# Attention and MLP on one core: q and k of seven batches by way of fp16 copies in DRAM and DMA transposes

## The chip, the cores and the metric

The kernel runs on one core of a Trainium2 chip. A core has TensorE (PE: matmuls, whose weight loads stand apart as PEld), VectorE (DVE), ScalarE (ACT), GpSimd (POOL) and SyncE (SP). They run side by side and wait for one another on semaphores. In this kernel SP and POOL issue the DMAs. The metric is the device time of one execution in microseconds (us), as the median of several runs.

## The reference

```python
# q, k, v: (8, 12, 448, 64) float32: batch, heads, tokens, head size
scores = scale * np.matmul(q, k.transpose(0, 1, 3, 2))       # scale = 1/8
m = np.max(scores, axis=-1, keepdims=True)
e = np.exp(scores - m)
attn = e / (np.sum(e, axis=-1, keepdims=True) + np.exp(-m) + 1e-09)
attn_out = np.matmul(attn, v)
x = attn_out.transpose(0, 2, 1, 3).reshape(3584, 768)
h = x @ w_in                                                 # (768, 2048)
r = np.maximum(h, 0.0)
out = (r * r) @ w_out                                        # (2048, 768), float32 out
```

This is attention whose softmax has one more term in its sum (the exp(-m), which is exp(0) after the shift), and then an MLP with a squared ReLU over all 3584 tokens.

## The kernel before

Work is cut by batch (8), in each batch by pair of heads (6, so 48 pairs in all), and in each pair by key group (4 of 112 tokens). A batch has 448 tokens. The natural tiles have 112 partitions, and partition p holds tokens 4p to 4p+3; key group kk is the tokens 4p+kk. All matmul operands are fp16, so POOL's loads cast from fp32 (`load`, L78); the first three pairs of q and k come uncast through SP (`load_raw`, L86), so that they come soon.

For the scores, q and k must lie with the head size on the partitions. `regroup` (L102) makes a copy on DVE, for three pairs at a time and for q and k each, that puts the two heads of a pair side by side (`flatq`, `flatk`, L109). `transposes` (L114) then turns one pair with eight TensorE transposes (four of q, four of k, L119) into a PSUM tile of the pool of two `mp` buffers, and one DVE copy brings it to SBUF (`qkt`, L121): head 0 on partitions 0 to 63, head 1 on 64 to 127.

For each key group, `scores` (L124) issues two matmuls, one for each head (L128: weights 112 columns of k, moving operand 448 columns of q; head 0 in the upper 64 rows of the array and head 1 in the lower), and one ACT exponential of both (`et`, L129). DVE sums the four key groups (`es`, L133, L136). `values` (L138) multiplies with v (L141), `row_sums` (L144) sums over keys on TensorE (L147) and takes the reciprocal on ACT by a logarithm and an exponential (L150, L151), and `normalise` (L154) writes the pair's rows of `xt` on DVE (L158).

`mlp` (L161) is a generator that yields after each matmul. Its first part makes 16 blocks of the hidden layer: six matmuls (L167) into an `mp` buffer, a ReLU on DVE (`rt`, L172) and a square on DVE (`g`, L174). Its second part multiplies with w_out (L182), brings each result to SBUF on ACT (`ot`, L186) and stores it from SP (L196). Blocks have 384 or 512 tokens in turn, so that block b needs the batches up to b.

The order is written out by hand: the scheduler is off (L58), and each engine runs its instructions as the program issues them. The loop over pairs (L251) issues the scores of pair i, two key groups, then the transposes of pair i+1, then 45% of this pair's share of the MLP of the batch before (`drain`, L233), then the other two key groups, and then values, row sums and normalise of pair i-1 with the rest of the share in between. The share is a sixth of a block. So the first half of each batch holds the first product (L167) and the second half the second (L182). `regroup` of pairs 3 to 5 comes at the end of pair 1, that of the next batch's pairs 0 to 2 at the end of pair 4 (L294 to L297).

Loads of batch b+1 are issued on POOL at the start of batch b (L258; batch 1's at the start of the kernel, in halves, between slices of w_in, L212 to L221). The q and k tiles have two buffers, so POOL waits for DVE's regroup; v waits for L141.

Of the kernel before, what the change touches and what calls it, by code (L numbers as in the profile page):

```python
# [15 lines left out]
def kernel(  # L16
# [9 lines left out]
    nc = tc.nc  # L26
# [8 lines left out]
    P = S // RUN  # L35

# [7 lines left out]
    nat = ctx.enter_context(tc.tile_pool(name="nat", bufs=2))  # L44
    raw = ctx.enter_context(tc.tile_pool(name="raw", bufs=1))
    flat = ctx.enter_context(tc.tile_pool(name="flat", bufs=2))
    qkt_pool = ctx.enter_context(tc.tile_pool(name="qkt", bufs=3))
# [23 lines left out]
    nats, flats, xts = {}, {}, {}  # L71

    def tiles_of(b):
        if b not in nats:
            nats[b] = {n: nat.tile([P, H, RUN, D], FP16, name=f"{n}n") for n in ("q", "k", "v")}
        return nats[b]

    def load(b, names, p0, p1):  # L78
        hs = slice(2 * p0, 2 * p1)
        for n in names:  # L80
            r = {"q": q_r, "k": k_r, "v": v_r}[n]
            nc.gpsimd.dma_start(out=tiles_of(b)[n][:, hs], in_=r[b, :, hs])  # L82

    raws = {}

    def load_raw(b, p0, p1):  # L86
        hs = slice(2 * p0, 2 * p1)
        for n, r in (("q", q_r), ("k", k_r)):
            t = raw.tile([P, 2 * (p1 - p0), RUN, D], FP32, name=f"{n}raw{p0}")
            nc.sync.dma_start(out=t, in_=r[b, :, hs])  # L90
            raws[n, b, p0] = t
# [10 lines left out]
    def regroup(b, p0, p1):  # L102
        hs = slice(2 * p0, 2 * p1)
        n = 2 * (p1 - p0)
        both = []
        for name in ("q", "k"):
            t = raws.pop((name, b, p0)) if (name, b, p0) in raws else nats[b][name][:, hs]
            f = flat.tile([P, RUN, H // 2, D], FP16, name=f"flat{name}")
            nc.vector.tensor_copy(f[:, :, 0:n, :], t.rearrange("p h t d -> p t h d"))  # L109
            both.append(f)  # L110
        for pr in range(p0, p1):
            flats[b, pr] = both, 2 * (pr - p0)

    def transposes(b, pr):  # L114
        both, h0 = flats.pop((b, pr))
        tp = m_psum.tile([128, 2, 512], FP16, name="mp")
        for i, t in enumerate(both):
            for s in range(RUN):
                nc.tensor.transpose(tp[:, i, P * s:P * s + P], t[:, s, h0:h0 + 2, :], ident[0:P, 0:P])  # L119
        qkt = qkt_pool.tile([128, 2, S], FP16, name="qkt")  # L120
        nc.vector.tensor_copy(qkt, tp[:, :, 0:S])  # L121
        return qkt

    def scores(qkt, et, kk):  # L124
        sp = s_psum.tile([P, 2, 512], FP32, name="sp")
        for h in range(2):
            r = slice(64 * h, 64 * h + 64)
            nc.tensor.matmul(sp[:, h, 0:S], qkt[r, 1, P * kk:P * kk + P], qkt[r, 0, :], start=True, stop=True)  # L128
        nc.scalar.activation(out=et[:, kk], in_=sp[:, :, 0:S], func=AF.Exp, scale=scale)  # L129
# [7 lines left out]

    def values(b, pr, et, xp, kk):  # L138
        vn = nats[b]["v"]
        for h in range(2):  # L140
            nc.tensor.matmul(xp[64 * h:64 * h + 64, 0:S], vn[:, 2 * pr + h, kk, :], et[:, kk, h, :],  # L141
                             start=(kk == 0), stop=(kk == RUN - 1))

    def row_sums(es):  # L144
        zp = xz_psum.tile([128, 512], FP32, name="zp")
        for h in range(2):
            nc.tensor.matmul(zp[64 * h:64 * h + 64, 0:S], ones, es[:, 0, h, :], start=True, stop=True)  # L147
        lnz = z_pool.tile([128, S], FP32, name="lnz")
        rcp = z_pool.tile([128, S], FP32, name="rcp")
        nc.scalar.activation(out=lnz, in_=zp[:, 0:S], func=AF.Ln, bias=one_b)  # L150
        nc.scalar.activation(out=rcp, in_=lnz, func=AF.Exp, scale=-1.0)  # L151
        return rcp
# [8 lines left out]
    def mlp(t0, n):  # L161
# [15 lines left out]
        for ts in range(n // 128):  # L177
# [13 lines left out]
            while c < end:  # L191
                b, t, p = c // S, c % S // P, c % P
                m = min(P - p, end - c)
                o = c + 128 - end
                rows = out[b * S:(b + 1) * S, :].rearrange("(p t) m -> t p m", t=RUN)
# [3 lines left out]


    load_raw(0, 0, 1)
    load_raw(0, 1, 3)
    load(0, "v", 0, 3)
    load(0, "qk", 3, 6)
    load(0, "v", 3, 6)
# [8 lines left out]
    load(1, "qkv", 0, 3)  # L214
    for i in range(3, 6):
        load_win(i, 8)
    load(1, "qkv", 3, 6)
# [28 lines left out]
    qkts, ets, ess = {}, {}, {}  # L246
    regroup(0, 0, 1)
    qkts[0] = transposes(*pairs[0])
    regroup(0, 1, 3)
    share = 0.0  # L250
    for i in range(NP + 1):  # L251
# [3 lines left out]
        if i < NP:  # L255
            b, pr = pairs[i]
            if pr == 0 and 0 < b and b + 1 < B:
                load(b + 1, "qkv", 0, 6)  # L258
            et = ets[i] = e_pool.tile([P, RUN, 2, S], FP16, name="et")
            es = ess[i] = e_pool.tile([P, 2, 2, S], FP16, name="es")  # L260
            scores(qkts[i], et, 0)
            scores(qkts[i], et, 1)
            if i + 1 < NP:
                qkts[i + 1] = transposes(*pairs[i + 1])
            drain(share * 0.45)
            scores(qkts[i], et, 2)
# [3 lines left out]
            scores(qkts[i], et, 3)  # L270
            qkts.pop(i)
        if i > 0:
            for kk in range(2 if not work and i < NP else 0, RUN):
                values(*pairs[i - 1], ets[i - 1], xp, kk)
            rcp = row_sums(ess.pop(i - 1))
# [17 lines left out]
        if i < NP:  # L293
            if pr == 1:  # L294
                regroup(b, 3, 6)
            if pr == 4 and b + 1 < B:
                regroup(b + 1, 0, 3)  # L297
# [31 lines left out]
```

## Time and profile before

| What | Value |
|---|---|
| Three runs | median 497.36 us (495.08 to 498.45) |
| Profiled execution, its own time | 497.45 us |
| Its span | 495.7 us |
| Mean granted TensorE clock | 0.978 |
| Exponentials of the scores, ACT (L129) | 192 of 913 ns, 165.3 us busy |
| First product, PE (L167) | 768 matmuls, 163.6 us busy |
| Second product, PE (L182) | 896 matmuls, 153.9 us busy |
| Scores, PE (L128) | 384 matmuls, 62.3 us busy |
| Transposes, PE (L119) | 384 matmuls, 19.0 us (q) and 19.1 us (k) busy |
| Copies of the transposed pairs, DVE (L121) | 48 of 621 ns, 29.8 us busy |
| DMA bytes, packets | 34.97 MB, 45665 |

"Busy" is the time in which at least one instruction of the kind ran; matmuls overlap, so the mean of one times the count is more. In a timeline row stand the start, the time taken, the engine, the line, the operation, the tiles written and read, the shape and the count of merged instructions; a bracket at the end gives the engine's idle time before and what ended it. A windows row gives the length of a stretch, the busy time of each engine with its instructions, the mean granted clock, the DMA engines' share and the bytes moved.

Seen from the starts of the pairs' scores, batches last 55.4 us (3 and 5), 60.6 us (2 and 4), 53.0 us (1, from 43.7 us), 61.4 us (6) and 59.2 us (7); the MLP of the last block runs alone after that, from 449.3 us to the end.

### The profile page before, as it was taken

The numbers are of one execution on the slowest core, as the hardware profiler recorded it, in microseconds if no ns is written. First come the engines' busy times: TensorE is split into PE (matmuls) and PEld (weight loads), VectorE is DVE, ScalarE is ACT, GpSimd is POOL, SyncE is SP. The second block draws the span as 40 slices with busy tenths as digits, with TensorE's granted clock in tenths as the row PEclk, the third lists the DMA queues.
The fourth block names the chain that finished last, engine by engine and source line by source line (L and its number), as shares of the span: only waits on it lengthen the run. The fifth ranks groups of instructions, "written<-read, shape, count | busy, mean of one in ns | idle before, by whom it ended". The sixth has DMA issues, their size and how long they took to land.

```text
span 495.7 us, 7052 instructions
## 1 busy us (share of the span) xinstructions
PE 448.1 (90%) x2912; PEld 221.9 (45%) x2912; DVE 280.8 (57%) x532; ACT 244.2 (49%) x345; POOL 35.5 (7%) x46
## 2 busy tenths in 40 slices
PE   1787789997999979997999988998999989999996
PEld 1333345543355534543355534553345544455453
DVE  2656766457853568457754466637684277635800
ACT  2688436663355635663365635565245663561011
POOL 6342100001000010001000010000000000000000
PEclk9998999999999989999999989999899998999999
DMA  9999990256112580144702545115001210021022
GB/s 184 197 197 206 205 184 7 65 87 86 26 33 65 88 110 3 33 68 66 99 1 64 79 79 75 34 32 89 0 2 33 63 33 0 1 65 32 1 62 67
DMA packets 45665, 34.97 MB, mean 71 GB/s; under 512 B 1600, under 2 KB 42048, under 8 KB 45632
## 3 DMA queue, kind: packets, MB, share of 16 engines
q0 software_dynamic: 39744, 22.12, 33.1%
q1 hardware_dynamic: 5888, 12.39, 8.5%
q8 instruction: 23, 0.38, 0.3%
q14 instruction: 10, 0.08, 0.0%
HBM read 45.61 MB, written 11.01 MB: 114 GB/s over the span
## 4 chain that ended last, share of the span: by engine, by line
PE 73%; DVE 20%; ACT 3%; DMA 2%; issue 1%; SPq 0%; ACTq 0%
PE mp L182 30%; PE mp L167 20%; PE xp L141 9%; PE sp L128 8%; DVE rt L172 6%; PE mp L119 4%; DVE es L133 4%; DVE g L174 4%; DMA kraw<-in_k_dram 2%; PE zp L147 2%; DVE xt L158 2%; ACT et L129 2%; DVE es L136 2%; DVE qkt L121 2%; DVE flatq L109 1%
## 5 line engine op out<-in xcount | busy, mean ns | idle before, releaser
L129 ACT ACTIVATE et<-sp 112x896 f16<-112x896 f32 x192 | 165.3, 913 | 167.9 <-PE sp L128 167.9
L167 PE MATMUL mp<-xt,win 128*128 128x384 f16 (+1 forms) x768 | 163.6, 363 | 6.5 <-DVE rt L172 3.5
L182 PE MATMUL mp<-wout,g 128*128 128x512 f16 (+1 forms) x896 | 153.9, 326 | 0.4
L167 PEld LDWEIGHTS <-win 128*128 128x128 f16 x768 | 74.5, 100 | 86.2 <-issue 27.9
L182 PEld LDWEIGHTS <-g 128*128 128x128 f16 x896 | 84.9, 98 | 61.0 <-issue 9.2
L172 DVE TENSOR_SCALAR rt<-mp 128x384 f16<-128x384 f32 (+1 forms) x128 | 79.6, 622 | 56.4 <-PE mp L167 53.2
L133 DVE TENSOR_TENSOR es<-et 112x896 f16<-112x896 f16 x96 | 59.1, 622 | 83.0 <-ACT et L129 82.8
L128 PE MATMUL sp<-qkt 64*112 64x448 f16 x384 | 62.3, 395 | 4.3 <-ACT et L129 3.6
L186 ACT ACTIVATE ot<-mp 128x512 f32<-128x512 f32 (+1 forms) x56 | 27.3, 487 | 72.8 <-PE mp L182 72.1
L174 DVE TENSOR_TENSOR g<-rt 128x384 f16<-128x384 f16 (+1 forms) x128 | 50.1, 392 | 4.4
L141 PE MATMUL xp<-et,vn 112*64 112x448 f16 x384 | 49.7, 377 | 0.0
L121 DVE COPY qkt<-mp 128x896 f16<-128x896 f16 x48 | 29.8, 621 | 32.3 <-PE mp L119 32.3
L119 PE MATMUL mp<-ident,flatq 112*128 112x112 f16 x192 | 19.0, 226 | 28.9 <-DVE flatq L109 20.6
L128 PEld LDWEIGHTS <-qkt 64*112 64x112 f16 x384 | 19.2, 130 | 42.3 <-issue 40.0
L150 ACT ACTIVATE lnz<-zp,one_b 128x448 f32<-128x448 f32 x48 | 30.7, 640 | 4.1 <-PE zp L147 4.1
L158 DVE TENSOR_TENSOR xt<-xp,rcp 128x448 f16<-128x448 f32 x48 | 29.7, 619 | 4.8 <-ACT rcp L151 4.4
L119 PEld LDWEIGHTS <-flatq 112*128 112x128 f16 x192 | 11.5, 102 | 46.3 <-DVE flatq L109 29.5
L136 DVE TENSOR_TENSOR es<-es 112x896 f16<-112x896 f16 x48 | 29.9, 623 | 1.2
L141 PEld LDWEIGHTS <-vn 112*64 112x64 f16 x384 | 17.5, 111 | 24.5 <-issue 18.2
L151 ACT ACTIVATE rcp<-lnz 128x448 f32<-128x448 f32 x48 | 27.7, 577 | 1.5
L82 POOL DMA_DIRECT2D vn<-in_v_dram x10 | 9.0, 898 | 220.5 <-PE zp L147 217.2
L119 PE MATMUL mp<-ident,flatk 112*128 112x112 f16 x192 | 19.1, 228 | 2.6 <-DVE flatk L109 2.0
(20 smaller groups left out, 83.3 us busy)
## 6 DMA issues: line engine op xcount, KB each, us to landing
qn<-in_q_dram POOLq DMA_DIRECT2D x6, 672.0 KB, 7.8
kn<-in_k_dram POOLq DMA_DIRECT2D x6, 672.0 KB, 10.5
vn<-in_v_dram POOLq DMA_DIRECT2D x6, 672.0 KB, 8.9
win<-in_moe_w_in_dram POOLq DMA_DIRECT2D x8, 384.0 KB, 15.4
wout<-in_moe_w_out_dram POOLq DMA_DIRECT2D x4, 768.0 KB, 18.9
out_dram<-ot SPq DMA_DIRECT2D x8, 336.0 KB, 2.8
out_dram<-ot SPq DMA_DIRECT2D x8, 288.0 KB, 2.7
out_dram<-ot SPq DMA_DIRECT2D x8, 240.0 KB, 2.8
```

What stands on the lines that cost most here:

```text
L119: nc.tensor.transpose(tp[:, i, P * s:P * s + P], t[:, s, h0:h0 + 2, :], ident[0:P, 0:P])
L121: nc.vector.tensor_copy(qkt, tp[:, :, 0:S])
L128: nc.tensor.matmul(sp[:, h, 0:S], qkt[r, 1, P * kk:P * kk + P], qkt[r, 0, :], start=True, stop=True)
L129: nc.scalar.activation(out=et[:, kk], in_=sp[:, :, 0:S], func=AF.Exp, scale=scale)
L133: nc.vector.tensor_add(es[:, c], et[:, cs.start], et[:, cs.start + 1])
L136: nc.vector.tensor_add(es[:, 0], es[:, 0], es[:, 1])
L141: nc.tensor.matmul(xp[64 * h:64 * h + 64, 0:S], vn[:, 2 * pr + h, kk, :], et[:, kk, h, :], start=(kk == 0), stop=(kk == RUN - 1))
L158: nc.vector.tensor_mul(xts[b // 2][:, pr, c:c + S], xp[:, 0:S], rcp)
L167: nc.tensor.matmul(hp[:, 0:n], win[:, dc, fb * 128:(fb + 1) * 128], xt[:, dc, x0:x0 + n], start=(dc == 0), stop=(dc == DCH - 1))
L172: nc.vector.tensor_scalar(out=rt[:, 0:n], in0=hp[:, 0:n], scalar1=0.0, scalar2=None, op0=ALU.max)
L174: nc.vector.tensor_mul(g[:, 0:n], rt[:, 0:n], rt[:, 0:n])
L182: nc.tensor.matmul(op[:, 0:n1 - n0], gt[fb][:, ts * 128:(ts + 1) * 128], wout[:, fb, n0:n1], start=(fb == 0), stop=(fb == NFFB - 1))
```

## The change

Batch 0 keeps TensorE's transposes; its regroup is now one pair at a time, into buffers of the `g` pool, and its transposed q and k go to one tile `qk` of the whole batch. For each of batches 1 to 7, `stage` has POOL copy all of q and all of k of a batch from DRAM to DRAM with a cast to fp16, the k copy beginning 64 elements (one token) earlier than the batch. `transposed_loads` has SP load these copies with DMA transpose: a row of 128 elements is two tokens, so that even tokens land on partitions 0 to 63 and odd ones on 64 to 127. There are three loads for a batch: q, k, and k shifted by one token, so that each parity of keys is to be had on both halves of the partitions. `qk` has two buffers, one for each of two batches.

The scores of a key group of batches 1 to 7 are then four matmuls of 224 columns (each head, even and odd queries) in place of two of 448; their weights are read with a step of two columns. The tokens of a batch stand in the order even, then odd, through `et`, `es`, `xt` and the output, whose stores are cut accordingly (37 stores in place of 49). Issue order: batch 1's copies stand behind three slices of w_in on POOL, its v in one load behind three more; later batches' copies and v are issued where the loads were. The transposed loads of batch b+1 are issued on SP at the end of pair 2 of batch b. TensorE has as many instructions as before: 336 transposes fewer and 336 score matmuls more.

```diff
+    COLS = H * S // 2 + 16
-    nat = ctx.enter_context(tc.tile_pool(name="nat", bufs=2))
-    raw = ctx.enter_context(tc.tile_pool(name="raw", bufs=1))
-    flat = ctx.enter_context(tc.tile_pool(name="flat", bufs=2))
-    qkt_pool = ctx.enter_context(tc.tile_pool(name="qkt", bufs=3))
+    nat = ctx.enter_context(tc.tile_pool(name="nat", bufs=1))
+    v_pool = ctx.enter_context(tc.tile_pool(name="v", bufs=2))
+    qk_pool = ctx.enter_context(tc.tile_pool(name="qk", bufs=2))
...
+    HSD = H * S * D
+    FRONT, TOTAL = D, HSD + 16 * 2 * D
+
+    def stage(b):
+        for n, t in (("q", q), ("k", k)):
+            st = nc.dram_tensor(f"stage_{n}{b}", (TOTAL,), FP16, kind="Internal").ap()
+            stages[n, b] = st
+            src = t.rearrange("b h s d -> (b h s d)")
+            lo = b * HSD - FRONT
+            hi = min(lo + TOTAL, B * HSD)
+            m = (hi - lo) // 1024 * 1024
+            for x, y in ((lo, lo + m), (lo + m, hi)):
+                if y > x:
+                    w = min(y - x, 1024)
+                    nc.gpsimd.dma_start(out=st[x - lo:y - lo].rearrange("(r w) -> r w", w=w),
+                                        in_=src[x:y].rearrange("(r w) -> r w", w=w))
...
+    def transposed_loads(b):
+        qk = qks[b] = qk_pool.tile([128, 3, COLS], FP16, name="qk")
+        for i, n, x, c in ((0, "q", FRONT, H * S // 2), (1, "k", FRONT, H * S // 2), (2, "k", 0, COLS)):
+            nc.sync.dma_start(
+                out=qk[:, i, 0:c],
+                in_=stages[n, b][x:x + c * 2 * D].rearrange("(r c) -> r c", c=2 * D),
+                transpose=True,
+            )
+
+    def regroup(pr):
+        for j, name in enumerate("qk"):
+            f = g_pool.tile([128, 512], FP16, name=f"g{2 * pr + j}")
...
+        qk = qks[b]
+        if b == 0:
...
+        else:
+            for h in range(2):
+                for odd in range(2):
+                    r = slice(64 * odd, 64 * odd + 64)
+                    c = (2 * pr + h) * (S // 2)
+                    kc = c + kk // 2
+                    which = 1
+                    if kk % 2 != odd:
+                        which = 2
+                        kc += kk % 2
+                    nc.tensor.matmul(sp[:, odd, h * (S // 2):(h + 1) * (S // 2)],
+                                     qk[r, which, kc:kc + 2 * P - 1:2], qk[r, 0, c:c + S // 2],
+                                     start=True, stop=True)
...
+    def of_head(e, b, h):
+        if b == 0:
+            return e[:, h, :]
+        return e.rearrange("p o (h c) -> p h o c", h=2)[:, h]
...
-    load(1, "qkv", 0, 3)
+    stage(1)
     for i in range(3, 6):
         load_win(i, 8)
-    load(1, "qkv", 3, 6)
+    load_v(1, 0, 6)
...
-                load(b + 1, "qkv", 0, 6)
+                stage(b + 1)
+                load_v(b + 1, 0, NPAIR)
...
-            if i + 1 < NP:
-                qkts[i + 1] = transposes(*pairs[i + 1])
+            if i + 1 < NPAIR:
+                transposes(i + 1)
...
-            if pr == 1:
-                regroup(b, 3, 6)
-            if pr == 4 and b + 1 < B:
-                regroup(b + 1, 0, 3)
+            if i + 2 < NPAIR:
+                regroup(i + 2)
+            if pr == 2 and b + 1 < B:
+                transposed_loads(b + 1)
```

## The prediction

> **What bounds the kernel now.** I read the page first, engines and chain:
>
> ```profile
> PE 448.1 (90%) x2912; PEld 221.9 (45%) x2912; DVE 280.8 (57%) x532; ACT 244.2 (49%) x345; POOL 35.5 (7%) x46
> ...
> PE 73%; DVE 20%; ACT 3%; DMA 2%; issue 1%; SPq 0%; ACTq 0%
> ```
>
> TensorE is busy for 90% of the span, and the chain that ended last is PE with pieces of DVE in it. So two things pay: PE instructions that go, and PE idle time that DVE causes. The windows of two stretches, for block 4 (first matmuls, with PE clock) and block 3 (second matmuls), separate them:
>
> ```profile
> core 0: us, PE busy (x) PEld busy (x) DVE busy (x) ACT busy (x) POOL busy (x), PEclk, DMA share, GB/s
> 281.70:310.80 29.10, 25.30 (x165) 12.59 (x163) 20.42 (x43) 13.12 (x18) 1.86 (x2) 0.94 0.58 84
> 251.70:273.30 21.60, 21.60 (x153) 11.67 (x151) 9.93 (x18) 11.79 (x18) 0.00 (x0) 1.00 0.14 38
> ```
>
> While the second product runs, PE has no gap at all. While the first runs, 3.8 us of 29.1 are idle, and the clock is at 0.94. The timeline of PE and then of DVE shows where:
>
> ```profile
> 289.22 0.59 PE L128 MATMUL sp<-qkt 64*112 64x448 f16 x4
> 291.94 0.37 PE L119 MATMUL mp<-ident,flatq 112*128 112x112 f16 x4 [2.13 <-DVE flatq L109]
> 292.41 0.37 PE L119 MATMUL mp<-ident,flatk 112*128 112x112 f16 x4
> 292.61 4.43 PE L167 MATMUL mp<-xt,win 128*128 128x384 f16 x15
> ```
> ```profile
> 289.94 0.55 DVE L172 TENSOR_SCALAR rt<-mp 128x384 f16<-128x384 f32 x1
> 290.52 0.36 DVE L174 TENSOR_TENSOR g<-rt 128x384 f16<-128x384 f16 x1
> 290.80 0.62 DVE L158 TENSOR_TENSOR xt<-xp,rcp 128x448 f16<-128x448 f32 x1
> 291.33 0.55 DVE L109 COPY flatq<-qn 112x1536 f16<-112x1536 f16 x1
> 291.80 0.55 DVE L109 COPY flatk<-kn 112x1536 f16<-112x1536 f16 x1
> ```
>
> In the third pair of a batch PE wants to transpose, but DVE regroups q and k only behind its other work. PE waits 2.13 us. The same wait stands in all seven batches 1 to 7 (PE timeline: before 60.04, 115.58, 175.99, 231.54, 291.94, 347.52 and 408.82 us). The 15 matmuls behind it take 4.43 us; two batches earlier, with no wait before, the same number takes 2.60:
>
> ```profile
> 165.71 2.60 PE L167 MATMUL mp<-xt,win 128*128 128x384 f16 x15
> ```
>
> So a drop of the granted clock follows the wait. Transposes with nothing to wait for cost this:
>
> ```profile
> 312.00 0.58 PE L128 MATMUL sp<-qkt 64*112 64x448 f16 x4
> 312.51 0.37 PE L119 MATMUL mp<-ident,flatq 112*128 112x112 f16 x4
> 312.72 0.36 PE L119 MATMUL mp<-ident,flatk 112*128 112x112 f16 x4
> 312.92 2.54 PE L182 MATMUL mp<-wout,g 128*128 128x512 f16 x11
> ```
>
> Eight fill 312.51 to 312.92, 0.41 us. Four score matmuls of 448 columns fill 0.51 us.
>
> **The parts and their prices.** (1) Transposes go for pairs 6 to 47: 42 x 0.41 = -17.2 us. They lie on PE's path in both stretches.
>
> (2) The wait goes: 7 x 2.13 = -14.9. The flatk four start 0.47 us after the flatq four (291.94, 292.41), against 0.21 undisturbed: 7 x 0.26 = -1.8. What is late next is DVE itself: without the regroup it still has rt, g and xt to do until 291.33, and PE, with two mp buffers, can run about one and a half hidden blocks ahead (six matmuls, about 1 us each). I put back 0.4 us a batch, the size of the other mp waits in this stretch: +2.8. Bounds: 0, and the whole 16.7 if DVE holds PE just the same. DVE's load speaks for the low end: its 20.4 us busy in the 29.1 lose three qkt copies (0.62 each) and two regroup copies (0.55), so 17.4 is left, against a PE that needs some 22.3 (25.3 busy, less 1.2 of transposes and 1.8 of clock).
>
> (3) The clock: the 15 matmuls after the wait took 4.31, 4.40, 4.43 and 3.98 us in batches 1, 3, 5, 7 against 2.60, so 1.7 + 1.8 + 1.8 + 1.4; batch 6's third pair is 0.9 longer than those of batches 2 and 4. Together -7.6. Bounds: 0 (another gap trips it) to -7.6; I take all, since the only gap over 2 us in these batches is the one that goes.
>
> (4) PE waits 0.25 us for the qkt copy once a batch, because the transposes take one of the two mp buffers: -1.8. The 42 copies (0.62) and 22 of the 34 regroup copies leave DVE; beyond what is counted above they run beside PE and are worth nothing.
>
> (5) Scores of batches 1 to 7 become four matmuls of 224 columns instead of two of 448, in the same two row halves. The 15 matmuls from 165.71 to the next scores at 168.24 stream 15 x 384 columns in 2.53 us, 2.28 a ns. At that rate the four of 448 (a set: two key groups) would take 0.79 us one after another and 0.39 two at a time; they take 0.51. So they run two at a time, with 0.12 for the first load and the change of tile shape. So columns streamed stay the same. Weight loads double (336 more, with a step of two). Low bound 0; high bound, every further load exposed as the first is (a part of the 0.12, say 0.05): 84 sets (two for each of 42 pairs) x 3 x 0.05 = 12.6 us. I take +1, since L119 pays no visible load between matmuls of only 112 columns.
>
> [...]
>
> (6) Batch 0 keeps TensorE. Its regroup goes pair by pair, so three more iterations wait for DVE's xt and two copies before the transposes (up to about 1 us each), while the wait of 1.93 us before batch 1's transposes (39.57) goes. I call it even, within 3 us.
>
> (7) DMA. POOL's q and k loads of batches 1 to 7 (14 tensors) turn into casts from DRAM to DRAM of the same source bytes. They wait for no buffer that DVE frees (POOL now waits 61.2 us for flatq, which holds up nothing), so they are issued earlier, about a batch ahead. Batch 1's v becomes one load behind three of win: 5.7 MB into the queue, so at about 37 us plus what the transposed loads take, needed near 52.8, where L141 of batch 1's first pair runs. SP gets 21 transposed loads of 688 KB. Each waits for its copy and for the scores of two batches before; behind it on SP stand only stores, which wait for ScalarE anyway and are hidden behind two ot buffers. In steady state 2.1 MB of transposed loads a batch have about 50 us, as the copy runs a batch ahead. The first batch has less: the queues are full then.
>
> ```profile
> GB/s 184 197 197 206 205 184 7 65 87 86 26 33 65 88 110 3 33 68 66 99 1 64 79 79 75 34 32 89 0 2 33 63 33 0 1 65 32 1 62 67
> ```
>
> POOL's queue moves about 197 GB/s written. Before batch 1's copies stand 2.5 MB of POOL's loads (four of 336 KB, three of 384) and SP's 1.3 MB; with 1.35 MB of copies and the start, they land at about 28 to 30 us (5.2 MB / 197 + 2). Batch 1's scores begin at 43.66 us now. Nothing in the trace transposes by DMA. From below: by source bytes, 394 GB/s (the casts read twice what they write), 5.2 us for the three. From above, short of a collapse: the window of 12 to 40 us shows 10977 packets, 16 x 28 / 10977 = 41 ns each per engine; if each 256-byte row costs that, 3 x 168 x 41 ns = 20.7 us. Shared evenly with POOL's loads both double: 10.4 to 41 us, ending at 38 to 70, so a stall of 0 to 27 us, once. Nearest is the middle, moving bytes at 197 GB/s: 10.5, shared 21, ending near 47 to 49 if the first starts at 26. I take +3.
>
> [...]
>
> **Sum.** 495.7 - 17.2 - 14.9 - 1.8 + 2.8 - 7.6 - 1.8 + 1.0 + 0 + 3.0 = 459.2 us of span. The profiled execution took 497.45, 1.75 over its span, and equals the median of the runs (497.36). So 461 us.
>
> **Rivals.** A, the first batch starves: rows of 256 bytes cost 41 ns, batch 1 waits 12 to 27 us instead of 3: 470 to 485. For it: DMA is full for the first 74 us. Against it: only if arbitration gives SP's queue no more than half.
>
> B, DVE takes PE's place while the first product runs: the 16.7 and 7.6 us stay, less the 2.8 put back: 461 + 21.5 = 482. Against it: 17.4 us of DVE work in some 23.
>
> C, the transposed loads set the pace, and it is slower. They need 2.1 MB a batch; once that takes longer than a batch's PE work (about 50 us), the span is 26 + 7T + the last batch and tail (52 + 46). It equals 495.7 at T = 53 us, 17.7 us a load or 105 ns per row and engine. If a row is written in many small pieces, at 150 ns say, T is 76 and the time 26 + 529 + 98 + 1.75 = 655. Against it: the worst packet price seen is 41 ns, so it takes 2.6 times that. For it: nothing here shows such a load.
>
> D, the change does not do what it says: PE still waits as in B, and the scores' further loads are all exposed (11.6 more): 494, no change that can be told.
>
> **How the numbers follow.** The main case 0.62, A 0.10, B 0.07, C 0.17, D 0.04. The main case reaches from 451 (batch 0 gains 3, no stall, no DVE wait, no price of the scores) down to 449 for what these durations round, and up to 470, where A begins. The range 446 to 487 takes in the main case, A and B: 0.79. A measurement of this kernel tells about 1% from no change. Faster 0.79, same 0.04, slower 0.17; the main case's own range is 449 to 470.
>
> **What would show it.** Right: no L119 after 40 us; third pairs of 9.5 to 11 us instead of 13.3; score sets (eight matmuls) still 0.51 to 0.55 us; transposed loads landing within 25 us; odd batches near 49 us, even ones near 56, from 55.4 and 60.6. Wrong: PE waiting for DMA at the start of each batch (C) or of batch 1 alone (A); rt waits of 2 us at the third pair (B); score sets of 0.7 us (D).

## The result, and the profile after

The changed kernel is slower: 517.50 us (four runs, 514.19 to 520.34) against 497.90 (four runs of the kernel before, on the same chip), a ratio of 1.0394 with a 95% interval of 1.031 to 1.0477. The forecast was 461, and faster. The profiled execution took 517.9 us, with a span of 515.5; line numbers from here on are those of the changed kernel (scores of batches 1 to 7 L164, first product L211, second L226, copies to DRAM L112, transposed loads L121). The changed kernel issues 42 stores of the output where the kernel before issues 56.

The page first: engines, slices, DMA totals and the chain.

```profile
PE 426.3 (83%) x2912; PEld 219.7 (43%) x2912; DVE 242.0 (47%) x468; ACT 244.9 (48%) x345; POOL 29.4 (6%) x47
...
PE   2773000079999999999999999999999999999996
...
PEclk9998555569999999999999999999999999999999
...
DMA packets 84384, 49.50 MB, mean 96 GB/s; under 512 B 58688, under 2 KB 80320, under 8 KB 83904
...
PE 63%; DVE 15%; DMA 9%; another core or an unknown queue 8%; SPq 1%; POOL 1%; issue 1%; ACT 0%; POOLq 0%
```

TensorE did become cheaper: 426.3 us busy instead of 448.1, DVE 242.0 instead of 280.8. From the tenth slice on PE is at 9 in every slice but the last, where the kernel before falls to 7 or 8 time and again. But slices 5 to 8 (a slice is 12.9 us) are zeros, the granted clock falls to 0.5 there, and the chain has 9% of DMA and 8% of an unknown queue, where it had 2% of DMA. The waits of PE name the gap:

```profile
engine line waited for: us in total, times, longest us
PE sp L164 <- DMA qk<-stage_k: 59.9, 2, 42.7
...
PE mp L211 <- DVE rt L216: 5.7, 15, 0.6
```

Two waits at the start of batch 1 hold 59.9 us; no other wait for a transposed load is in the whole span, and 515.5 - 59.9 = 455.6. The PE timeline shows them, and SP's and POOL's timelines what was under way:

```profile
44.35 0.36 PE L191 MATMUL zp<-es,ones 112*64 112x448 f16 x2
61.91 0.43 PE L164 MATMUL sp<-qk 64*112 64x224 f16 x1 [17.20 <-DMA qk<-stage_k]
...
105.06 0.99 PE L164 MATMUL sp<-qk 64*112 64x224 f16 x7 [42.72 <-DMA qk<-stage_k]
```

```profile
26.18 7.07 SPq L121 DMA_TRANSPOSE qk<-stage_q  x1
33.29 66.05 SPq L121 DMA_TRANSPOSE qk<-stage_k  x2
100.74 4.58 SPq L121 DMA_TRANSPOSE qk<-stage_q  x1
105.41 5.79 SPq L121 DMA_TRANSPOSE qk<-stage_k  x2
```

```profile
40.16 0.52 POOL L112 DMA_DIRECT2D stage_q<-in_q_dram  x1 [2.48 <-DMA win<-in_moe_w_in_dram]
45.32 0.51 POOL L112 DMA_DIRECT2D stage_k<-in_k_dram  x1 [4.64 <-DMA vn<-in_v_dram]
```

Batch 1's three transposed loads (called T1 from here) start at 26.18 us, as forecast. The second one lands shortly before 62 us and the third shortly before 105, and not at 47 to 49. Meanwhile POOL issues batch 2's copies at 40 and 45 us. Batch 2's own transposed loads (100.74, 105.41) take 4.6 and 5.8 us on SP's queue. The copies are no earlier than what they replace: the kernel before issues batch 2's loads of q and k, beside which no transposed load stood, at 39 and 41 us:

```profile
39.19 1.34 POOL L82 DMA_DIRECT2D qn<-in_q_dram  x1 [1.71 <-DVE xt L158]
40.52 0.94 POOL L82 DMA_DIRECT2D kn<-in_k_dram  x1
```

After 112 us the kernel runs as forecast. Windows of a stretch with first products (batch 5) and of one with second products (batch 4):

```profile
core 0: us, PE busy (x) PEld busy (x) DVE busy (x) ACT busy (x) POOL busy (x), PEclk, DMA share, GB/s
320.50:349.10 28.60, 27.18 (x199) 14.16 (x198) 20.87 (x45) 15.27 (x21) 1.30 (x3) 1.00 1.00 157
289.60:312.40 22.80, 22.80 (x163) 12.50 (x160) 9.75 (x18) 12.65 (x20) 0.00 (x0) 1.00 0.12 35
```

PE idles 1.4 us of 28.6 where it idled 3.8 of 29.1, and the clock is 1.00 where it was 0.94. The third pair, where the 2.13 us wait and the 15 matmuls of 4.43 us behind it stood (the granted clock was 0.61 over those 4.43 us of the kernel before, and is 1.00 here from 327.58 to 331.59):

```profile
327.58 0.59 PE L164 MATMUL sp<-qk 64*112 64x224 f16 x8
328.11 0.50 PE L211 MATMUL mp<-xt,win 128*128 128x384 f16 x2
328.90 1.14 PE L211 MATMUL mp<-xt,win 128*128 128x384 f16 x6 [0.29 <-DVE rt L216]
330.29 1.30 PE L211 MATMUL mp<-xt,win 128*128 128x384 f16 x7 [0.26 <-DVE rt L216]
```

Batches from start to start of their scores, in us (for batch 7 its first five pairs), before and after; the last row is of the kernel that holds every copy, told of below:

| Kernel | 0 | 1 | 2 | 3 | 4 | 5 | 6 | 7 |
|---|---|---|---|---|---|---|---|---|
| before | 36.7 | 53.1 | 60.6 | 55.4 | 60.6 | 55.4 | 61.5 | 46.8 |
| changed | 55.1 | 91.3 | 55.0 | 49.1 | 55.0 | 49.1 | 55.0 | 41.1 |
| every copy held | 38.4 | 48.3 | 55.0 | 49.0 | 55.0 | 49.0 | 55.0 | 41.1 |

(The stall begins in the last pair of batch 0, whose time reaches to batch 1's first score.)

So the question is why T1, 2.07 MB, took 79 us. Counting the trace's single DMA packets by when they start gives this, with the mean time of one in brackets. SP's queue holds the rows of T1 (256 bytes each, 8080 of them for a batch), POOL's the others: 512 bytes for w_in and v, 1536 for w_out, 21632 for batch 2's copies. (Moving a stretch by some nanoseconds moves a count by a few.)

```
us        rows of 256 B    512 B         1536 B        21632 B
36-40     869 (31 ns)      870 (59 ns)
44-48     889 (32 ns)      799 (59 ns)   69 (137 ns)
56-60     456 (31 ns)                    447 (134 ns)
60-64     432 (31 ns)                    449 (134 ns)
68-72     178 (72 ns)                    74 (547 ns)   10 (1757 ns)
80-84     58 (495 ns)                    13 (1006 ns)  8 (2088 ns)
88-92     227 (325 ns)                   8 (564 ns)    6 (1612 ns)
100-104   332 (189 ns)                                 2 (1612 ns)   (287 of these rows behind the last packet)
104-108   3959 (20 ns)
108-112   3828 (20 ns)
```

Beside POOL's queue a row went for each packet of POOL's, at 512 bytes as at 1536: 870 packets to 869 rows, 447 to 456. Alone, from 104 us on, rows run at 3959 in 4 us: 253 GB/s, and that only where nothing else moves. Between 64 and 104 us far fewer rows come: few packets of either kind are under way, and all are slow. The end of that stretch, in quarters of a microsecond:

```
POOL's packets under way, 97 to 104 us: 97.07-98.68, 98.69-100.30, 100.33-101.94, 101.95-103.56 (21632 B each)
rows from 97.00: 38 7 0 0 | 0 0 1 17 | 0 0 0 0 | 0 14 18 0 | 0 0 0 1 | 12 0 0 0 | 0 0 27 260 | from 104.00: 281 275 263
```

Four packets, one after the other and so presumably on one of the 16 engines, let 13 to 32 rows through in each change of packets, about one or two for each engine if they lie evenly, and hardly any between (0 or 1 in a quarter); 0.2 us after the last of them the rate is 260 in a quarter. So would rows do that go on in step over the engines, at the pace of the engine with the most foreign packets: a conjecture, which the last experiment takes up.

### The profile page after: what moved, and what is told of

Read it like the earlier page. It is cut to its first block, busy times and chain, and to the rows that moved or that the text cites. A ratio compares the mean times of both kernels' runs of the same rounds, so it can differ in the third digit from the quotient of the medians.

```text
span 515.5 us, 7005 instructions
## 1 busy us (share of the span) xinstructions
PE 426.3 (83%) x2912; PEld 219.7 (43%) x2912; DVE 242.0 (47%) x468; ACT 244.9 (48%) x345; POOL 29.4 (6%) x47
## 3 DMA queue, kind: packets, MB, share of 16 engines
q0 software_dynamic: 21456, 22.18, 28.6%
## 4 chain that ended last, share of the span: by engine, by line
PE 63%; DVE 15%; DMA 9%; another core or an unknown queue 8%; SPq 1%; POOL 1%; issue 1%; ACT 0%; POOLq 0%
PE mp L226 29%; PE mp L211 17%; PE sp L164 8%; PE xp L185 7%; DVE rt L216 6%; DMA qk<-stage_k 6%; DMA stage_q<-in_q_dram 4%; DVE es L171 3%; DVE g L218 3%; PE zp L191 2%; SPq L121 1%; DVE es L174 1%; DVE xt L202 1%; POOL win L89 0%
## 5 line engine op out<-in xcount | busy, mean ns | idle before, releaser
L211 PE MATMUL mp<-xt,win 128*128 128x384 f16 (+1 forms) x768 | 158.4, 354 | 7.0 <-DVE rt L216 5.7
L226 PE MATMUL mp<-wout,g 128*128 128x512 f16 (+1 forms) x896 | 154.0, 326 | 0.4
L226 PEld LDWEIGHTS <-g 128*128 128x128 f16 x896 | 84.2, 98 | 63.6 <-issue 10.0
L211 PEld LDWEIGHTS <-win 128*128 128x128 f16 x768 | 71.8, 98 | 85.9 <-issue 24.9
L164 PE MATMUL sp<-qk 64*112 64x224 f16 x672 | 51.8, 273 | 60.6 <-DMA qk<-stage_k 59.9
L164 PEld LDWEIGHTS <-qk 64*112 64x112 f16 x672 | 32.2, 130 | 91.5 <-DMA qk<-stage_k 60.6
L194 ACT ACTIVATE lnz<-zp,one_b 128x448 f32<-128x448 f32 x48 | 30.7, 640 | 4.6 <-PE zp L191 4.6
L191 PE MATMUL zp<-es,ones 112*64 112x448 f16 x96 | 18.2, 376 | 0.0
L139 PE MATMUL mp<-ident,g 112*128 112x112 f16 x48 | 5.7, 297 | 14.4 <-DVE g L132 9.2
L152 PE MATMUL sp<-qk 64*112 64x448 f16 x48 | 12.9, 580 | 2.9 <-ACT et L167 2.2
L139 PEld LDWEIGHTS <-g 112*128 112x128 f16 x48 | 4.2, 139 | 17.9 <-DVE g L132 17.0
## 6 DMA issues: line engine op xcount, KB each, us to landing
win<-in_moe_w_in_dram POOLq DMA_DIRECT2D x8, 384.0 KB, 19.8
wout<-in_moe_w_out_dram POOLq DMA_DIRECT2D x4, 768.0 KB, 49.1
```

The lines of the kernel that those rows point to most:

```text
L164: nc.tensor.matmul(sp[:, odd, h * (S // 2):(h + 1) * (S // 2)], qk[r, which, kc:kc + 2 * P - 1:2], qk[r, 0, c:c + S // 2], start=True, sto ...
L191: nc.tensor.matmul(zp[64 * h:64 * h + 64, 0:S], ones, of_head(es[:, 0], b, h), start=True, stop=True)
L211: nc.tensor.matmul(hp[:, 0:n], win[:, dc, fb * 128:(fb + 1) * 128], xt[:, dc, x0:x0 + n], start=(dc == 0), stop=(dc == DCH - 1))
L226: nc.tensor.matmul(op[:, 0:n1 - n0], gt[fb][:, ts * 128:(ts + 1) * 128], wout[:, fb, n0:n1], start=(fb == 0), stop=(fb == NFFB - 1))
```

## The experiments

Theory P: T1 runs at its own speed only alone; beside POOL's queue each row waits for one of POOL's packets, so the size and number of the packets that POOL has queued set T1's end; everything else in the prediction stands. Rival B: T1 is slow because of the bytes that compete for the engines, so that only fewer bytes help. Rival for the other terms: the forecast's gain in the batches isn't due to the causes named.

All ratios are against runs of the kernel before on the same chip (median 497.90 for the changed kernel, 498.37 for the last two kernels, 498.02 for the others). The waits are those of the profiled execution.

| Kernel | us, median | ratio, 95% interval | PE's wait for transposed loads, us |
|---|---|---|---|
| changed | 517.50 | 1.0394, 1.031 to 1.0477 | 59.9, batch 1 |
| batch 2's copies held | 488.52 | 0.9802, 0.9755 to 0.9848 | 30.7, batch 1 |
| all POOL loads held for T1 | 480.87 | 0.9643, 0.9593 to 0.9692 | 19.8, batch 2 |
| copies in 832-byte packets | 492.88 | 0.988, 0.9836 to 0.9925 | 34.0, batch 1 |
| before, regroup a pair earlier | 483.93 | 0.970, 0.9649 to 0.9751 | none exist |
| every copy held | 458.63 | 0.9195, 0.9157 to 0.9232 | 0 |
| batch 2's copies held, thin w_out | 479.38 | 0.961, 0.9556 to 0.9664 | 21.1, batch 1; 7.6, batch 2 |
| every copy held, regroup in three | 457.02 | 0.9161, 0.9121 to 0.9201 | 1.4, batch 2 |
| the same, v first | 457.96 | 0.9193, 0.9144 to 0.9242 | 2.4, batch 2 |
| every copy held, one copy more | 459.57 (one run) | | 0.9, batch 2 |

**Batch 2's copies held.** POOL copies three numbers out of the tile that T1 fills, and so waits for T1 before it issues batch 2's copies. T1 is issued where it was on SP.

```diff
+    def fence():
+        mark = consts.tile([1, 3], FP16, name="mark")
+        nc.gpsimd.tensor_copy(mark, qks[1][0:1, :, 0])
...
     stage(1)
+    qks[0] = qk_pool.tile([128, 3, COLS], FP16, name="qk")
+    transposed_loads(1)
...
         load_wout(i, 4)
+    fence()
...
-            if pr == 2 and b + 1 < B:
+            if pr == 2 and 0 < b and b + 1 < B:
```

> The changed kernel, but POOL issues batch 2's copies only when batch 1's three transposed loads have landed (POOL copies three numbers of them first); the loads of w_in, v and w_out stand beside them as before. Theory P (the queues take turns packet by packet, so a transposed load of 256-byte rows advances one row for each packet of POOL's queue, and the 21632-byte packets of batch 2's copies starve it most): by 64 us some 5700 of 8080 rows are through as before, the rest runs beside the tail of w_out and then alone at about 990 rows a us, so batch 1's first scores start near 68 us in place of 105, and the time falls by about 36 us to 482. Rival H (the transposed loads are slow beside any traffic, and the size of the packets does not matter): the load ends near 90 us or later and the time stays above 500.

Measured 488.52 us, 6 above the 482 expected. The wait is halved, 30.7 us, and the second half of it goes from 42.7 to 13.3:

```profile
62.98 0.43 PE L164 MATMUL sp<-qk 64*112 64x224 f16 x1 [17.43 <-DMA qk<-stage_k]
76.71 0.99 PE L164 MATMUL sp<-qk 64*112 64x224 f16 x7 [13.30 <-DMA qk<-stage_k]
```

Batch 2's copies cost 29 us of the stall. The rest is w_in, v and w_out: up to 64 us the counts are those of the changed kernel (442 packets of 1536 bytes to 450 rows in 56 to 60). T1 ended at 76 and not some 8 us earlier: from 64 to 76 us the rows came at 898, 527 and 1029 in 4 us, beside POOL's last 259 packets (190, 47 and 22). Why they came so slowly beside so few was not shown.

**All POOL loads held for T1.** The same wait, but right behind batch 1's copies, so that nothing of POOL's runs beside T1. The rest of w_in, batch 1's v and w_out come after.

```diff
     stage(1)
+    qks[0] = qk_pool.tile([128, 3, COLS], FP16, name="qk")
+    transposed_loads(1)
+    fence()
     for i in range(3, 6):
         load_win(i, 8)
...
-            if pr == 2 and b + 1 < B:
+            if pr == 2 and 0 < b and b + 1 < B:
```

> The changed kernel, but POOL holds everything behind batch 1's copies (five slices of w_in, batch 1's v, w_out, batch 2's copies) until batch 1's transposed loads have landed. Theory P: the three loads run alone, at 253 GB/s as batch 2's did between 104 and 112 us, and land near 38 us, before batch 1 wants them at 44.7 us; no stall, w_out lands near 66 us, before it is wanted at about 72; time 455 to 460, as the steady batches (49 and 55 us) say. Rival W (the held weights come too late and PE waits for them instead): 465 to 480, with PE waiting for win or wout. Rival H: as the loads run nearly alone, no difference from P.

Measured 480.87 us, 21 us above what was expected, and the loss was in a place that no theory had. T1 landed at 39 us and batch 1 had no wait. But batch 2 waited. POOL's, SP's and PE's timelines:

```profile
39.09 0.26 POOL L249 COPY mark<-qk 1x3 f16<-1x3 f16 x1 [27.34 <-DMA qk<-stage_k]
49.78 0.52 POOL L112 DMA_DIRECT2D stage_q<-in_q_dram  x1 [1.30 <-DMA win<-in_moe_w_in_dram]
53.25 0.51 POOL L112 DMA_DIRECT2D stage_k<-in_k_dram  x1 [2.94 <-DMA vn<-in_v_dram]
57.53 0.50 POOL L112 DMA_DIRECT2D stage_q<-in_q_dram  x1 [0.94 <-DMA win<-in_moe_w_in_dram]
61.78 0.50 POOL L112 DMA_DIRECT2D stage_k<-in_k_dram  x1 [3.75 <-DMA wout<-in_moe_w_out_dram]
```

```profile
76.04 26.62 SPq L121 DMA_TRANSPOSE qk<-stage_q  x1
102.76 8.15 SPq L121 DMA_TRANSPOSE qk<-stage_k  x2
```

```profile
110.63 0.43 PE L164 MATMUL sp<-qk 64*112 64x224 f16 x1 [17.92 <-DMA qk<-stage_k]
112.91 0.99 PE L164 MATMUL sp<-qk 64*112 64x224 f16 x7 [1.85 <-DMA qk<-stage_k]
```

POOL went on to issue batch 3's copies at 57.5 and 61.8 us, behind batch 2's, and they ran beside batch 2's transposed loads: the q load alone occupies SP's queue for 26.6 us. It is the same collision one batch later.

**Copies in 832-byte packets.** Order of the changed kernel; only the copies' rows are cut, so that a packet has 832 bytes (1024 in the last batch) instead of 21632. Bytes stay the same, so this tells P from B.

```diff
-            for x, y in ((lo, lo + m), (lo + m, hi)):
-                if y > x:
-                    w = min(y - x, 1024)
...
+            w = 416 if hi - lo == TOTAL else 512
+            for j in range(2):
+                nc.gpsimd.dma_start(out=st[0:m].rearrange("(r j w) -> r j w", j=2, w=w)[:, j],
+                                    in_=src[lo:lo + m].rearrange("(r j w) -> r j w", j=2, w=w)[:, j])
```

> The changed kernel, but each copy from DRAM to DRAM is two, of alternate pieces of 416 elements (832 bytes written; 512 elements in the last batch), so that no packet is larger than 1536 bytes; order and waits are those of the change. Theory P: the rows no longer meet packets of 21632 bytes; after 64 us the last 2300 rows run at 110 to 215 rows a us and end at 75 to 85 us; time 488 to 500. Rival D (copies from DRAM to DRAM collide with the transposed loads whatever their packets): batch 1 starts as late as now, 510 to 525.

Measured 492.88 us, within what P expects. With the same bytes in the same order the wait falls from 59.9 to 34.0 us:

```profile
61.34 0.43 PE L166 MATMUL sp<-qk 64*112 64x224 f16 x1 [15.22 <-DMA qk<-stage_k]
80.56 0.99 PE L166 MATMUL sp<-qk 64*112 64x224 f16 x7 [18.79 <-DMA qk<-stage_k]
```

Rows again come one for one: from 72 to 76 us 616 rows beside 568 packets of 832 bytes and 23 of 1536. It is the size of the packets, and B falls.

**The kernel before, regroup a pair earlier.** The other side of the prediction: is the wait for `flatq` at the third pair worth what terms 2 and 3 say? In the kernel before, and there alone, the regroup of pairs 3 to 5 moves from the end of pair 1 to that of pair 0.

```diff
-            if pr == 1:
+            if pr == 0:
                 regroup(b, 3, 6)
```

> The kernel before, with one edit: the regroup of pairs 3 to 5 is issued at the end of a batch's first pair instead of its second. Theory: the wait of 2.13 us at the third pair of batches 1 to 7 and the clock drop behind it come only from where the regroup stands in DVE's order; without it 14.9 + 1.8 + 7.6 us less up to 2.8, so 473 to 478. Rival: DVE is the bound of that half in any case, and PE waits elsewhere for it: 488 to 497.

Measured 483.93 us, 14 us less than before and not 20 to 25. The 2.13 us wait and the clock's drop are gone (the clock is 0.9 or more from the sixth slice on, and 1.00 from 278 to 306 us), but two smaller waits stand in the third pair instead:

```profile
284.66 0.36 PE L119 MATMUL mp<-ident,flatq 112*128 112x112 f16 x4 [0.73 <-DVE rt L172]
284.85 0.36 PE L119 MATMUL mp<-ident,flatk 112*128 112x112 f16 x4
285.05 0.49 PE L167 MATMUL mp<-xt,win 128*128 128x384 f16 x2
286.12 2.27 PE L167 MATMUL mp<-xt,win 128*128 128x384 f16 x13 [0.58 <-DVE qkt L121]
```

The transposes still take one of the two mp buffers and DVE still has to empty it. So 14 of the 39 us that the change is worth without its stall (next kernel) can be had with one moved line; the rest was seen only with the transposes and their copies off PE and DVE.

**Every copy held.** As with all POOL loads held for T1, and from batch 2 on POOL also waits for a batch's transposed loads before it issues the next batch's copies.

```diff
             if pr == 0 and 0 < b and b + 1 < B:
+                if b > 1:
+                    fence(b)
                 stage(b + 1)
                 load_v(b + 1, 0, NPAIR)
```

> As e2 (POOL holds all behind batch 1's copies until batch 1's transposed loads have landed), and in each later batch POOL also holds the next batch's copies until the current batch's transposed loads have landed. In e2 batch 2's first scores still waited 18 us, because batch 3's copies ran beside batch 2's transposed loads. Theory P: with no packet of 21632 bytes beside any transposed load, no batch waits for DMA; from e2's own starts 44.4 + 48.3 + 55.0 + 49.0 + 55.0 + 49.0 + 55.0 + 99.4 = 455 us of span, time 457 (455 to 460), ratio about 0.92. Rival L (the copies now start too late and each batch waits for its transposed loads): some us more in each of batches 3 to 7, 465 or more.

Measured 458.63 us, ratio 0.9195. This is the changed kernel without its stall, and it beats both. POOL's timeline shows its waits; SP's shows T1; and the page shows PE:

```profile
39.58 0.59 POOL L250 COPY mark<-qk 1x3 f16<-1x3 f16 x1 [27.23 <-DMA qk<-stage_k]
...
91.90 0.18 POOL L250 COPY mark<-qk 1x3 f16<-1x3 f16 x1 [34.88 <-DMA qk<-stage_k]
```

```profile
26.53 3.66 SPq L121 DMA_TRANSPOSE qk<-stage_q  x1
30.24 7.03 SPq L121 DMA_TRANSPOSE qk<-stage_k  x2
```

```profile
PE 425.3 (93%) x2912; PEld 219.2 (48%) x2912; DVE 241.8 (53%) x468; ACT 245.0 (54%) x345; POOL 31.7 (7%) x53
...
PE   2677899999999999999999999999999999999996
...
PEclk9996799999999999999999999999999999999999
```

T1 alone takes 26.5 to about 39 us. PE has no wait for a transposed load in the whole span, nor one for w_in, w_out or v, so what POOL holds back is not missed.

**Batch 2's copies held, thin w_out.** The order of "batch 2's copies held", and w_out cut by columns in three parts, so that its packets are of 512 bytes and not 1536. By P T1 gains, by bytes it can't.

```diff
-        w = NFFB // n
-        nc.gpsimd.dma_start(out=wout[:, i * w:(i + 1) * w, :], in_=wout_r[:, i * w:(i + 1) * w, :])
+        w = DM // n
+        nc.gpsimd.dma_start(out=wout[:, :, i * w:(i + 1) * w], in_=wout_r[:, :, i * w:(i + 1) * w])
```

> As e1 (only batch 2's copies are held), but w_out is loaded in three parts of 256 columns, so that its packets are 512 bytes written in place of 1536, for the same bytes. Theory P (one packet of each queue in turn): beside w_out the transposed loads advance at the 215 to 240 rows a us that they had beside w_in's 512-byte packets, in place of 112; from 48 us, with some 3700 rows to go, they end near 64 to 66 us in place of 75, and the time falls by 8 to 10 us from e1's 488.5, to 478 to 481. Rival B (the queues share by bytes or by time): the size of POOL's packets changes nothing, 487 to 490.

Measured 479.38 us, as P has it: three runs are between 478.5 and 479.9, and the ratio is theirs. The profiled execution took 488.89 and also waits 7.6 us at batch 2, so its trace is used for T1 alone. There T1 is through at 66 us instead of 76, and rows and packets go one for one to the end: 951 packets of 512 bytes to 963 rows from 56 to 60 us, where "batch 2's copies held" had 442 of 1536 to 450.

**Every copy held, regroup in three.** Term 6: batch 0's regroup in two groups (pairs 0 to 2 ahead of the loop, pairs 3 to 5 at the end of pair 1) in place of one pair at a time.

```diff
+    regroup(2)
...
-            if i + 2 < NPAIR:
-                regroup(i + 2)
+            if i == 1:
+                for later in range(3, NPAIR):
+                    regroup(later)
```

> As e5, but in batch 0 the regroup copies of pairs 1 and 2 are issued together and those of pairs 3 to 5 together at the end of pair 1, as in the kernel before, in place of one pair at a time. The change's batch 0 reached its last pair at 40.5 us (e2: 38.9) where the kernel before did at 36.7. Theory: it is DVE's order that costs this (each iteration's transposes wait for the copies behind normalise), so 2 to 4 us come back against e5. Rival: batch 0 is bound by its loads, no difference from e5 (within 1 us).

Measured 457.02 us against 458.63, with intervals that overlap: inconclusive. In the profiled execution, which at 458.71 us was the slowest of the six, batch 1 starts 3.3 us earlier (41.9 against 45.2; with batch 0 as it was, two other kernels start it at 44.4 and 43.3, so the gain is 1.4 to 3.3). But the second interval between its pairs is 11.67 us instead of 8.88, and v is what is late:

```profile
54.57 0.95 PE L185 MATMUL xp<-et,vn 112*64 112x448 f16 x8 [1.64 <-DMA vn<-in_v_dram]
```

**The same, v first.** Batch 1's v is loaded directly behind the wait, ahead of the held slices of w_in.

```diff
+    load_v(1, 0, 6)
     for i in range(3, 6):
         load_win(i, 8)
-    load_v(1, 0, 6)
```

> The regrouping of batch 0 with batch 1's v loaded ahead of the held slices of w_in. If the wait for v at 54 us is what ate the gain of the regrouping (second interval of batch 1 11.7 us against 8.9, and the clock drop behind it), the second interval returns to about 9 us, and the time is 2 to 3 us below the run before it: 454 to 455.5. Rival: the slices of w_in come late in v's place, a wait of PE for them stands in batch 1, and the time stays at 457.

Measured 457.96 us: what neither expected. The wait for v is gone, and the second interval is back at 8.88 us, and no wait for w_in has come in its place. But batch 2, which batch 1 now reaches at 90.41 us instead of 93.46, waits for its transposed loads:

```profile
90.41 0.30 PE L164 MATMUL sp<-qk 64*112 64x224 f16 x1
93.10 0.99 PE L164 MATMUL sp<-qk 64*112 64x224 f16 x7 [2.39 <-DMA qk<-stage_k]
94.03 3.71 PE L226 MATMUL mp<-wout,g 128*128 128x512 f16 x15
```

These loads are issued at 76.31 to 77.33 us in all three kernels and are through by 91.9 to 94.8, since their copies stand behind everything that POOL held back for T1. So an earlier batch 1 meets the next wait in this order of issue; batch 3 begins at 148.5 to 149.7 us in all three. The 15 matmuls behind the wait take 3.71 us instead of 2.56; behind the gap in the kernel before it was 4.43 instead of 2.60.

**Every copy held, one copy more.** A test of the step "in step over the engines": 17 more packets of 21632 bytes, from v to a scratch in DRAM that nothing reads, on POOL's queue behind batch 1's copies.

```diff
     transposed_loads(1)
+    aside = nc.dram_tensor("aside", (17, 12032), FP16, kind="Internal").ap()
+    far = v.rearrange("b h s d -> (b h s d)")[0:17 * 12032].rearrange("(r w) -> r w", r=17)
+    nc.gpsimd.dma_start(out=aside[:, 0:10816], in_=far[:, 0:10816])
     fence(1)
```

> The version that holds every copy, with one more copy on POOL's queue beside batch 1's transposed loads: 17 packets of 21632 bytes into a scratch in DRAM that nothing reads. If the rows of a transposed load go on together over all DMA engines (theory S), a few large packets on few engines slow all rows: some tens to a few hundred rows in 4 us while the copy runs instead of 2500 to 2800, and batch 1's first scores wait for it, 5 to 20 us. If each engine takes its own rows by itself (rival I), the rows run at over 2000 in 4 us at first, only those of the engines concerned are late, and a wait at batch 1 is no longer than the packets of one engine, under 5 us.

One run, 459.57 us. As a stall it failed: 16 of the packets ran beside one another before T1 had begun in earnest, so batch 1 did not wait, and neither theory's time is tested. The packets themselves still bear on it. The last one, 28.05 to 29.66 us, is the only one under way after 28.92. Rows started in each quarter of a microsecond:

```
from 28.00: 156 136 86 36 | from 29.00: 18 9 7 150 | from 30.00: 285 283 282 285
```

With this single packet under way all rows together die down to 7 in a quarter, and they are back when it ends at 29.66. But this is the start of a load, and a load's start looks like this by itself: the second load of "the same, v first", with no packet of another queue under way, begins at 31.68 with 78, 109, 173, 219, 147, 34, 28 and 229 rows in its first quarters. So this run does not decide.

Two other traces do, in the midst of a load. There one packet of 16384 bytes of the instruction queue is under way, and no other packet but the rows: from 90.04 to 91.14 us in "the same, v first", and from 375.09 to 376.24 in the changed kernel. Rows started in each quarter:

```
from 90.00: 269 160 10 0 | from 91.00: 4 9 9 109 | from 92.00: 283 284
from 375.00: 242 265 75 2 | from 376.00: 1 8 9 10 | from 377.00: 236 287
```

If one packet is on one of the 16 engines, which no record shows, engines that went by themselves would have kept 15 of 16 of the rows. The rows return 0.6 to 0.8 us after the packet's end. With no other packet under way or ended less than 1 us before, the middle of a load (from 2.25 us after its first row to 0.5 us before its last) never falls below 277 rows in a quarter, in eight of the traces. So the stretch of the changed kernel from 97 to 103.6 us is not an accident of that place.

## Why the prediction was wrong, point by point

**The step that failed is (7)**, in the words "Shared evenly with POOL's loads both double: 10.4 to 41 us, ending at 38 to 70, so a stall of 0 to 27 us, once. Nearest is the middle". The stall came once, at batch 1, and was 59.9 us. Three things were wrong in it:

- "Shared evenly" was taken by time. The queues shared by packets: 869 rows of 256 bytes to 870 of POOL's packets of 512, 456 to 447 of 1536. Copies in packets of 832 bytes in place of 21632 took 26 us off the stall; with batch 2's copies held, w_out in packets of 512 in place of 1536 took 9 us off the time.
- Beside a single packet of another queue the rows of a load all but stopped: 0 to 10 in a quarter of a microsecond beside one of 16384 bytes, against some 280. This nothing in the trace of before could have shown. That the rows wait for the slowest engine, and that this made the stretch from 64 to 104 us slower than turns taken by each engine for itself, is the author's reading; no record names an engine.
- The copies from DRAM to DRAM were not priced as a neighbour of T1. The working has them "issued earlier, about a batch ahead", because no buffer of DVE's holds them. They were not: batch 2's were issued at 40.16 and 45.32 us, where the kernel before issued its loads at 39.19 and 40.52, and batch 3's, with all POOL loads held for T1, at 57.53 and 61.78, where the kernel before had 60.28 and 61.20. What was new is that T1 stood beside batch 2's copies, with their packets of 21632 bytes. Holding these copies alone took 29 us off.

The size alone: T1 by itself takes about 12 us (26.5 to 39), against a taken 10.5. With POOL's queue held back, the span is 455.6 us; the sum without its 3 us of stall gives 456.2.

**Rivals.** A had the right mechanism, batch 1 alone starving, and named its condition ("only if arbitration gives SP's queue no more than half"), but priced it at 12 to 27 us by the same even sharing, and gave it 0.10. C asked for 105 ns a row and engine all the way; between 80 and 84 us a row did take 495 ns, but only in the start. Later the same collision is there and hidden: batch 3's q load, beside batch 4's copies, occupies SP's queue from 160.91 us for 13.61, and is needed at 208. B and D are refuted by the third pair (waits of 0.29 and 0.26 us) and by the score sets. No rival joined A's mechanism with a price past the break-even: from 459.2 of span, 3 of them stall, 39.5 us of stall sufficed to make the kernel slower.

**The other terms.** The forecast of (1) to (5) together was -39.5 us. In the kernel that holds every copy, batches 1 to 7 (for 7 five pairs) are 40.8 us shorter by the table above, and the last pair with what follows 0.8: -41.6. These 2.1 us more than forecast make up for the 1.6 by which batch 0 ends later there, so the closeness of the whole sum is in part luck.

- (1) to (4): odd batches 49.05 us after, even ones 55.03; forecast "near 49" and "near 56". Only their sum is tested, not each price. The removed wait and the clock's drop are not from the transposes' absence alone: moving one regroup gave 14 us in the kernel before.
- (2), the 0.4 us a batch put back: 0.29 + 0.26 = 0.55 in batch 5.
- (3): the clock is 1.00 in the stretches that had 0.94.
- (5): a set of eight score matmuls of 224 columns takes 0.52 us (row below), where four of 448 took 0.51. The further weight loads cost at most 84 x 0.01 = 0.8 us; the +1 was right. The later matmuls of the set start two at a time, 96 ns a pair (319.62, 319.71, 319.81), so 48 ns each.

```profile
319.48 0.59 PE L164 MATMUL sp<-qk 64*112 64x224 f16 x8
320.00 2.61 PE L211 MATMUL mp<-xt,win 128*128 128x384 f16 x15
```

- (6): where batch 1 does not stall, batch 0 ends between 0.3 us earlier and 1.6 later (43.34, 44.40 and 45.22 in three kernels, against 43.66), within the 3 allowed. Grouping the regroup gains 1.4 to 3.3 us there, which later waits for loads take back.

The sum with the stall as measured is 459.2 - 3 + 59.9 = 516.1 of span, against 515.5.

## What to carry to other kernels

When a change makes a transfer urgent that was not there before, list what other queues have under way beside it: large transfers that were harmless there can now hold up the kernel, as batch 2's copies did here (holding them back took 29 us off). Price a transfer of many small rows beside another queue by the other queue's packets (rows per engine times the time of one packet, an estimate that gives 3.2 of the 4 us from 36 and 3.8 of the 4 from 56 here; and more beside large packets, where one of 16384 bytes left 0 to 10 rows in a quarter of a microsecond), not by bytes; and if it is needed soon, hold the other queue back until it has landed. Here six such waits, one for each of batches 1 to 6, turned 4% slower into 8% faster.

## What the runs showed of the hardware

- A transposed load and POOL's queue took turns one packet each: in 4 us 870 packets of 512 bytes to 869 rows, 447 of 1536 to 456, and 568 of 832 with 23 of 1536 to 616. Equal counts alone would fit turns of several packets each too; 13 to 32 rows for each 21632-byte packet (97 to 104 us) do not, if they lie evenly over the 16 engines: the turn was one or two rows. Where many such packets are under way at once (164 to 170 us, batch 3's loads beside batch 4's copies) it is 12 to 18 rows beside 14 to 17 packets in 2 us.
- With one packet of 16384 bytes of another queue under way in the midst of a load, 0 to 10 transposed rows started in a quarter of a microsecond instead of some 280 (two traces). The cause stays open: that the rows go on in step over the engines was not shown. The packets' records do not name their engine, so that the four packets from 97 us on shared one engine is read from their following one another without overlap.
- Alone, transposed rows ran at 253 GB/s over 4 us, and 285 in a quarter of a microsecond is 292 GB/s; the difference is the start of each load, where the rows are thin for up to some 2 us (28 to 229 in a quarter from 31.68 us on in "the same, v first"). The three loads of a batch, with the gaps between them, took about 12 us (26.5 to 39).
